# Four of eight convolution blocks per chunk: from the matrix engine to GpSimd, ScalarE and VectorE

## The chip, the core and the metric

The kernel runs on one core of a Trainium2 chip. A core has five engines, each with an instruction queue of its own that is worked off in order: TensorE (PE in the profile; its weight loads are the row PEld), VectorE (DVE), ScalarE (ACT), GpSimd (POOL) and SyncE (SP), which issues most of the transfers. The engines work on SBUF; TensorE writes its results to PSUM, which has eight banks of 512 fp32 values per partition. The metric is the device time of one execution in microseconds (us).

## The reference

Windowed attention for eight batches, eight heads, 576 positions, head width 64; behind it a feed-forward layer with a three-tap convolution along the sequence that gates the hidden units:

```
scores = (q @ k.T) / sqrt(64), masked to |i - j| <= 32
x = softmax(scores) @ v                      # (8, 576, 512) after the heads are put side by side
h = relu(x @ w_in)                           # (8, 576, 1024)
conv[s] = w0*h[s-1] + w1*h[s] + w2*h[s+1]    # per hidden unit, zeros outside
out = (h * sigmoid(conv)) @ w_out            # (8, 576, 512), fp32
```

## The kernel before, in words

The feed-forward part is cut into twelve chunks `c` of 384 positions; three chunks make two batches. A chunk has eight blocks `m` of 128 hidden units (partitions) by 384 positions. Each block goes through four steps: `ph` on TensorE (four matmuls with `w_in`, into a PSUM bank), `relu` on ScalarE (PSUM to the SBUF tile `hT`, with a factor 0.5), the convolution `pc` on TensorE (three matmuls whose weights are diagonal matrices `diag_w`, one for each tap, into another bank), then `tanh` on ScalarE in place in that bank and `gate` on VectorE (tanh plus one, times `hT`, into `gT`). Three groups `py` of eight matmuls then make the chunk's output, ScalarE copies each (`y`) and SyncE stores it. Chunks 0 and 1 are worked in halves of 192 positions.

Attention of batch `b` runs beside the chunks of the batches before it. GpSimd casts the loaded q, k and v to bf16 (`qb`, `kb`, `ve`), TensorE transposes q and k, ScalarE and VectorE copy these out (`qT`, `kT`), VectorE makes a shifted copy of v (`vo`, eight copies a batch), TensorE makes the scores, ScalarE the exponentials (`attn`), VectorE multiplies by the mask, TensorE multiplies with v, VectorE normalises (`rec`, `xn`), and for batches 2 to 7 a transposing DMA makes `xT`, the input of `ph`.

The order on every queue is fixed when the kernel is built. A `Planner` walks through all operations with costs given by hand and due times ("want"), takes on each engine the one that can start first and, among equals, the one due first, hands out the eight PSUM banks ("p"), and records the order. `shared` marks operations that it does not let run on DVE and POOL at once: all of POOL's, the mask multiplications and the `vo` copies. Chunk `c` is due at `S2 + (c - 2) * PC`; a batch is due `MO` or `ME` ahead of a chunk; `LD` spaces the loads. These times only sort the queues: on the chip every instruction starts when its own inputs and buffers are there. All calls go through a recording helper, so every instruction has line L209 in the profile (L212 in the changed file): operations are told apart by their tiles.

Of the kernel before, what the change touches and what calls it, by code (L numbers as in the profile page):

```python
# [10 lines left out]
FP32 = mybir.dt.float32  # L11
BF16 = mybir.dt.bfloat16
AF = mybir.ActivationFunctionType
ALU = mybir.AluOpType
# [12 lines left out]
class Planner:  # L27
# [110 lines left out]
def kernel(  # L138
# [21 lines left out]
    scale = 1.0 / float(D) ** 0.5  # L160
    CH = 2 * S // 3
    HW = CH // 2
    PAD = 32
    RP = S // 64
    NCH = 3 * B // 2
    ROWS = 2

    pp = ctx.enter_context(tc.tile_pool(name="pp", bufs=1))
    psum = ctx.enter_context(tc.tile_pool(name="psum", bufs=1, space=bass.MemoryType.PSUM))

# [14 lines left out]
    gT_pp = [pp.tile([128, MB, CH], BF16, name=f"gT{i}") for i in range(3)]  # L185
    rec_pp = [pp.tile([128, 8], FP32, name=f"rec{i}") for i in range(6)]
    y_pp = [pp.tile([128, d_model], FP32, name=f"y{i}") for i in range(6)]
    w_pp = [pp.tile([128, 1024], FP32, name=f"wst{i}") for i in range(4)]
    w_in_sb = pp.tile([128, KC, d_ff], BF16, name="w_in_sb")
    w_out_sb = pp.tile([128, MB, d_model], BF16, name="w_out_sb")  # L190
    conv_w_sb = pp.tile([128, 3, MB], FP32, name="conv_w_sb")
# [6 lines left out]
    pf = [psum.tile([128, 512], FP32, name=f"pf{i}") for i in range(8)]  # L198
# [46 lines left out]
    for t_ in ve_pp:  # L245
# [4 lines left out]
    vector.memset(hT_pp[1][:, :, HW + 1:HW + 3], 0.0)  # L250
    vector.memset(hT_pp[2][:, :, CH + 1], 0.0)

    plan = Planner({"p": range(8), "y": range(6),
                    "rec": range(6), "wst": range(4)})
# [238 lines left out]
    def taps(c, m, part, kk):  # L493
        kind = c % 3
        step = HW + (2 if kind == 1 else 0)
        base = hT_pp[kind][:, m, kk:kk + HW]
        return bass.AP(
            base.tensor, base.offset + step * (part or 0),
            [list(base.ap[0]), [step, 2 if part is None else 1], [1, HW]],
        )  # L500

    def pc_mm(c, m, part, ps):
        n = CH if part is None else HW
        for kk in range(3):
            tensor.matmul(
                pf[ps[0]][:, 0:n], diag_w[:, kk, m, :], taps(c, m, part, kk),
                start=(kk == 0), stop=(kk == 2),
            )

    def tanh(c, m, part, ps):  # L510
        n = CH if part is None else HW
        scalar.activation(pf[ps[0]][:, 0:n], pf[ps[0]][:, 0:n], AF.Tanh, bias=0.0, scale=1.0)

    def gate(c, m, part, ps):
        n = CH if part is None else HW
        o0 = HW * (part or 0)
        vector.scalar_tensor_tensor(
            out=gT_pp[c % 3][:, m, o0:o0 + n].rearrange("p (i x) -> p i x", x=HW),
            in0=pf[ps[0]][:, 0:n].rearrange("p (i x) -> p i x", x=HW), scalar=1.0,
            in1=taps(c, m, part, 1), op0=ALU.add, op1=ALU.mult,  # L520
        )
# [24 lines left out]

    PL = 0.25
    NSH = 8
    MO, ME = 5.0, 7.0
    NACT = 3  # L550
    LD = 1.7
    PC = 18.0
    S2 = 54.0

    def chunk_at(c):
# [2 lines left out]
    held = plan.held  # L558

    def ps_of(key):  # L560
        return held[key, "p"]
# [212 lines left out]
                    dma=0.75)  # L774


    def xt_need(c, part):
        x0, x1 = cols_of(c, part)
        b0 = c // 3 * 2
        need = []  # L780
        for b in range(2):
            lo, hi = max(x0, b * S) - b * S, min(x1, (b + 1) * S) - b * S
            if hi > lo:
                need += [("xt", b0 + b, x) for x in range(lo // 128, (hi - 1) // 128 + 1)]
        return need

    parts = {0: (0, 1), 1: (0, 1)}
    for c in range(NCH):
        ps_ = parts.get(c, (None,))
        for m in range(MB):  # L790
            for part in ps_:
                n = cols_of(c, part)[1] - cols_of(c, part)[0]
                w = CH if part is None else HW
                if c == 0:
                    t = 17.0 + 1.7 * m + 0.55 * part
                elif c == 1 and part == 0:
                    t = 18.1 + 1.7 * m
                elif c == 1:
                    t = 34.0 + 1.2 * m
                else:  # L800
                    t = chunk_at(c) + m * PC / (MB + 0.5)
                gap = (3.4 if c == NCH - 1 else 2.4) if part is None else 1.0
                hk, ck = ("ph", c, m, part), ("pc", c, m, part)
                add(hk, "PE", t, KC * (n / 2400.0 + 0.003),
                    lambda ps, c=c, m=m, part=part: ph_mm(c, m, part, ps),
                    xt_need(c, part) + [("w", 0, m // 2, h) for h in range(2)]
                    + [("gate", c - 3, m, p) for p in (None, 0, 1)],
                    lat=PL, takes=[("p", 1)])
                add(("relu", c, m, part), "ACT", t + 0.1, act(n),
                    lambda c=c, m=m, part=part: relu(c, m, part, ps_of(("ph", c, m, part))),  # L810
                    [hk] + [("gate", c - 3, m, p) for p in (None, 0, 1)]
                    + [("pc", c - 3, m, p) for p in (None, 0, 1)],
                    gives=[("p", hk, 0)])
                add(ck, "PE", t + gap, 3 * (w / 2400.0 + 0.003),
                    lambda ps, c=c, m=m, part=part: pc_mm(c, m, part, ps),
                    [("relu", c, m, part), *[("diag", m, kk) for kk in range(3)]]
                    + [("py", c - 3, i) for i in range(3)]
                    + ([("relu", c, m, 0)] if part == 1 and c % 3 == 0 else []),
                    lat=PL, takes=[("p", 1)])
                add(("tanh", c, m, part), "ACT", t + gap + 0.1, act(w),  # L820
                    lambda c=c, m=m, part=part: tanh(c, m, part, ps_of(("pc", c, m, part))),
                    [ck])
                add(("gate", c, m, part), "DVE", t + gap + 0.2, dve(w),
                    lambda c=c, m=m, part=part: gate(c, m, part, ps_of(("pc", c, m, part))),
                    [("tanh", c, m, part)] + [("py", c - 3, i) for i in range(3)],
                    gives=[("p", ck, 0)])
        for i in range(3):
            need = []
            for part in ps_:
                lo, hi = (0, CH) if part is None else (HW * part, HW * part + HW)  # L830
                if lo < 128 * i + 128 and hi > 128 * i:
                    need += [("gate", c, m, part) for m in range(MB)]
            last = c == NCH - 1 and i == 2
            nx = 2 if last else 1
            t = chunk_at(c + 1) + (2.7 + 2.6 * i) * PC / (MB + 0.5)
            yk = ("py", c, i)
            add(yk, "PE", t, MB * (d_model / 2400.0 + 0.003), lambda ps, c=c, i=i: py_mm(c, i, ps),
                need + [("w", 1, x, h) for x in range(4) for h in range(2)]
                + ([("issue", ("pc", c + 1, MB - 1, None))] if (c, i) == (NCH - 2, 2) else []),
                lat=PL, takes=[("p", nx)])  # L840
# [50 lines left out]
```

## Time and profile before

| what | value |
|---|---|
| time, median of 3 runs (lowest to highest) | 254.32 us (253.74 to 255.44) |
| the profiled execution: its time | 256.92 us |
| the profiled execution: its span, first to last instruction | 255.2 us |
| mean granted TensorE clock | 0.993 |
| last normalisation of batch 3, 5, 7 starts at | 97.4, 155.3, 211.2 us |

The span falls into three parts. Up to about 53 us the loads of the weights and of the first batches set the pace. From there to about 212 us attention of batches 2 to 7 runs beside chunks 1 to 9; three chunks and two batches take 58 and 56 us in the two full rounds (98 to 156 and 156 to 212 us). From 212 us on only the last chunks are left. PE's busy time is modelled: a matmul's recorded length contains the pipeline, so the pace of the matrix engine is read from start to start.

### The profile page before, as it was taken

The numbers are of one execution on the slowest core, as the hardware profiler recorded it, in microseconds if no ns is written. First come the engines' busy times: TensorE is split into PE (matmuls) and PEld (weight loads), VectorE is DVE, ScalarE is ACT, GpSimd is POOL, SyncE is SP. The second block draws the span as 40 slices with busy tenths as digits, with TensorE's granted clock in tenths as the row PEclk, the third lists the DMA queues.
The fourth block names the chain that finished last, engine by engine and source line by source line (L and its number), as shares of the span: only waits on it lengthen the run. The fifth ranks groups of instructions, "written<-read, shape, count | busy, mean of one in ns | idle before, by whom it ended". The sixth has DMA issues, their size and how long they took to land.

```text
span 255.2 us, 7176 instructions
## 1 busy us (share of the span) xinstructions
PE 240.9 (94%) x2782; PEld 154.2 (60%) x2782; DVE 179.6 (70%) x425; ACT 183.7 (72%) x429; POOL 76.4 (30%) x94
## 2 busy tenths in 40 slices
PE   7978998699999999999899999999999999999994
PEld 6976997586655555655555555656555555555542
DVE  4499789999997864649998958847798764233130
ACT  5789999387777776787568676776877775676651
POOL 5637676955300003055550065100560000000000
PEclk9999999799999999999999999999999999999999
DMA  6999999996614427899944699424995213321123
GB/s 240 273 267 388 237 318 405 215 352 176 158 42 59 119 59 222 163 308 313 315 121 63 179 347 214 111 83 137 367 181 84 94 45 65 109 85 41 41 83 127
DMA packets 69590, 45.96 MB, mean 180 GB/s; under 512 B 53532, under 2 KB 55860, under 8 KB 69556
## 3 DMA queue, kind: packets, MB, share of 16 engines
q1 hardware_dynamic: 69520, 45.49, 63.9%
q8 instruction: 22, 0.36, 0.6%
q14 instruction: 12, 0.10, 0.1%
q10 hardware_dynamic: 36, 0.01, 0.0%
HBM read 32.52 MB, written 9.44 MB: 164 GB/s over the span
## 4 chain that ended last, share of the span: by engine, by line
PE 60%; DVE 21%; DMA 8%; ACT 6%; issue 2%; POOL 1%; SPq 0%; DVEq 0%; POOLq 0%; ACTq 0%
PE pf L209 60%; DMA qst<-in_q_dram 6%; DVE kT L209 4%; DVE gT L209 4%; DVE xn L209 3%; DVE attn L209 3%; DVE vo L209 3%; ACT attn L209 3%; DVE qT L209 2%; DMA vst<-in_v_dram 2%; POOL qb L209 1%; DVE rec L209 1%; ACT diag_w L209 1%; ACT y L209 1%; ACT vo L209 1%
## 5 line engine op out<-in xcount | busy, mean ns | idle before, releaser
L209 DVE SCALAR_TENSOR_TENSOR gT<-pf,hT 128x384 bf16<-128x384 f32 (+1 forms) x112 | 57.0, 518 | 40.6 <-ACT pf L209 39.6
L209 PE MATMUL pf<-xT,w_in_sb 128*128 128x385 bf16 (+3 forms) x448 | 79.3, 305 | 0.5 <-ACT xT L209 0.4
L209 PE MATMUL pf<-w_out_sb,gT 128*128 128x512 bf16 (+1 forms) x296 | 67.6, 373 | 0.0
L209 PE MATMUL pf<-hT,diag_w 128*128 128x384 bf16 (+1 forms) x336 | 64.0, 303 | 1.4 <-DVE gT L209 1.2
L209 ACT ACTIVATE hT<-pf 128x385 bf16<-128x385 f32 (+3 forms) x112 | 50.7, 467 | 13.1 <-PE pf L209 11.1
L209 ACT ACTIVATE pf<-pf 128x384 f32<-128x384 f32 (+1 forms) x112 | 50.3, 457 | 5.1 <-PE pf L209 3.4
L209 PEld LDWEIGHTS <-w_in_sb 128*128 128x128 bf16 x448 | 39.4, 98 | 19.1 <-issue 0.5
L209 ACT COPY y<-pf 128x512 f32<-128x512 f32 (+1 forms) x36 | 20.9, 579 | 39.0 <-PE pf L209 39.0
L209 PEld LDWEIGHTS <-gT 128*128 128x128 bf16 x296 | 28.5, 98 | 29.3
L209 POOL TENSOR_SCALAR qb<-qst 128x1152 bf16<-128x1152 f32 x16 | 19.0, 1186 | 83.3 <-DMA qst<-in_q_dram 80.9
L209 ACT ACTIVATE attn<-pf 128x512 bf16<-128x512 f32 (+1 forms) x96 | 41.2, 506 | 1.2 <-PE pf L209 0.9
L209 PEld LDWEIGHTS <-diag_w 128*128 128x128 bf16 x336 | 30.6, 97 | 18.0 <-DVE gT L209 2.0
L209 DVE TENSOR_TENSOR attn<-attn,mask 128x1152 bf16<-128x1152 bf16 x32 | 27.4, 856 | 11.4 <-ACT attn L209 11.2
L209 POOL TENSOR_SCALAR ve<-vst 128x512 bf16<-128x512 f32 x40 | 26.1, 662 | 16.9 <-PE pf L209 6.1
L209 DVE TENSOR_TENSOR xn<-pf,rec 128x320 bf16<-128x320 f32 (+1 forms) x68 | 28.5, 461 | 0.1
L209 DVE COPY vo<-ve 64x520 bf16<-64x520 bf16 x60 | 24.7, 411 | 2.3 <-POOL ve L209 0.7
L209 DVE CAST qT<-pf 128x512 bf16<-128x512 f32 (+1 forms) x32 | 21.6, 717 | 5.2 <-PE pf L209 5.2
L209 DVE CAST kT<-pf 128x512 bf16<-128x512 f32 (+1 forms) x32 | 22.1, 725 | 2.2 <-PE pf L209 2.1
L209 POOL TENSOR_SCALAR kb<-kst 128x1152 bf16<-128x1152 f32 x16 | 19.1, 1192 | 9.9 <-DMA kst<-in_k_dram 9.6
L209 PEld LDWEIGHTS <-attn 128*64 128x64 bf16 x640 | 13.5, 115 | 12.1 <-issue 5.8
L209 PE MATMUL pf<-ve,attn 128*64 128x65 bf16 x384 | 17.0, 202 | 2.2 <-DVE attn L209 1.6
L209 PEld LDWEIGHTS <-kT 64*128 64x128 bf16 x576 | 10.5, 95 | 12.0 <-issue 6.7
(40 smaller groups left out, 173.0 us busy)
## 6 DMA issues: line engine op xcount, KB each, us to landing
qst<-in_q_dram SPq DMA_DIRECT2D x16, 576.0 KB, 6.6
kst<-in_k_dram SPq DMA_DIRECT2D x16, 576.0 KB, 7.9
out_dram<-y SPq DMA_DIRECT2D x35, 256.0 KB, 2.4
vst<-in_v_dram SPq DMA_DIRECT2D x24, 256.0 KB, 6.0
vst<-in_v_dram SPq DMA_DIRECT2D x16, 192.0 KB, 5.1
wst<-in_moe_w_in_dram SPq DMA_DIRECT2D x4, 512.0 KB, 6.3
wst<-in_moe_w_out_dram SPq DMA_DIRECT2D x4, 512.0 KB, 7.0
xT<-xn SPq DMA_TRANSPOSE x30, 2.5
```

Of the source, the lines that this page charges most:

```text
L209: return lambda *args, **kwargs: fixed(do(*args, **kwargs))
```

## The change

In chunks 2 to 10 the convolution of blocks 0, 1, 3 and 4 is no longer done by matmuls. Blocks 0 and 3 go to GpSimd: five instructions in SBUF, a multiplication into `ca` and two times a multiplication into `cb` and an addition to `ca`, in fp32; ScalarE's tanh then reads `ca` and writes a PSUM bank. Blocks 1 and 4 get a PSUM bank at once: ScalarE writes tap 0 times `hT` into it, VectorE adds taps 1 and 2 with two scalar_tensor_tensor instructions in place, tanh and gate follow as before. Blocks 2, 5, 6, 7 and the chunks 0, 1 and 11 stay with the matmuls. Four numbers of the planner change as well: PC, MO, ME and LD.

```diff
+    NCA = 3
+    ca_pp = [pp.tile([128, CH], FP32, name=f"ca{i}") for i in range(NCA)]
+    cb_pp = [pp.tile([128, CH], FP32, name=f"cb{i}") for i in range(2)]
...
+    def conv_pool(c, m, step, a, b):
+
+        a, b = halves(ca_pp[a]), halves(cb_pp[b])
+        if step in (0, 1, 3):
+            kk = (step + 1) // 2
+            pool.tensor_scalar(
+                out=b if step else a, in0=taps(c, m, None, kk), scalar1=conv_w_sb[:, kk, m:m + 1],
+                scalar2=None, op0=ALU.mult,
+            )
+        else:
+            pool.tensor_tensor(out=a, in0=a, in1=b, op=ALU.add)
+
+    def conv_acc(c, m, kk, ps):
+
+        to, w_ = halves(pf[ps[0]]), conv_w_sb[:, kk, m:m + 1]
+        if kk == 0:
+            scalar.activation(to, taps(c, m, None, kk), AF.Copy, bias=0.0, scale=w_)
+        else:
+            vector.scalar_tensor_tensor(
+                out=to, in0=taps(c, m, None, kk), scalar=w_, in1=to, op0=ALU.mult, op1=ALU.add
+            )
...
-    MO, ME = 5.0, 7.0
+    MO, ME = 6.0, 6.0
...
-    LD = 1.7
-    PC = 18.0
+    LD = 2.0
+    PC = 15.5
...
+    POOL_LAG = 6.0
+    BY_POOL, BY_DVE = (0, 3), (1, 4)
+
+    def conv_by(c, m):
+        if c < 2 or c == NCH - 1:
+            return "PE"
+        return "POOL" if m in BY_POOL else "DVE" if m in BY_DVE else "PE"
...
+                    add(tk, "ACT", t + POOL_LAG, act(w),
+                        lambda ps, c=c, m=m, qk=qk: tanh(c, m, None, ps, ca_pp[held[qk[0], "ca"][0]]),
+                        [ck], takes=[("p", 1)], gives=[("ca", qk[0], 0)])
```

What the planner makes of it, at three places. First GpSimd's queue at the casts of batch 5, which fall beside chunks 4 and 5 (`hT_89` is chunk 4's, `hT_90` chunk 5's). Before, the casts stand alone:

```order
L209 TENSOR_SCALAR ve_74<-vst 128x8x64 x5
L209 TENSOR_SCALAR qb_70<-qst_61 128x2x9x64
L209 TENSOR_SCALAR kb_72<-kst_63 128x2x9x64
L209 TENSOR_SCALAR qb_71<-qst_62 128x2x9x64
L209 TENSOR_SCALAR kb_73<-kst_64 128x2x9x64
L209 TENSOR_SCALAR ve_75<-vst 128x8x64 x5
```

The same casts in the changed kernel:

```order
L212 TENSOR_SCALAR ca_108<-hT_89,conv_w_sb 128x384
L212 TENSOR_SCALAR qb_70<-qst_61 128x2x9x64
L212 TENSOR_SCALAR cb_109<-hT_89,conv_w_sb 128x384
L212 TENSOR_TENSOR ca_108<-ca_108,cb_109 128x384
L212 TENSOR_SCALAR kb_72<-kst_63 128x2x9x64
L212 TENSOR_SCALAR cb_110<-hT_89,conv_w_sb 128x384
L212 TENSOR_SCALAR qb_71<-qst_62 128x2x9x64
L212 TENSOR_TENSOR ca_108<-ca_108,cb_110 128x384
L212 TENSOR_SCALAR ve_75<-vst 128x8x64 x2
L212 TENSOR_SCALAR ca_106<-hT_90,conv_w_sb 128x384
L212 TENSOR_SCALAR kb_73<-kst_64 128x2x9x64
```

A convolution that needs five instructions now has three casts between them, each of which waits for a load of its own.

Second VectorE's queue at the first mask multiplication of batch 4, beside the gates of chunk 4 (`gT_92`). Before:

```order
L209 TENSOR_TENSOR attn_82<-attn_82,mask 128x1152
L209 SCALAR_TENSOR_TENSOR gT_92<-pf_119,hT_89 128x384
L209 TENSOR_TENSOR attn_82<-attn_82,mask 128x1152
L209 COPY vo_76<-ve_74 64x520 x2
L209 SCALAR_TENSOR_TENSOR gT_92<-pf_120,hT_89 128x384
L209 COPY vo_76<-ve_74 64x520 x3
```

And in the changed kernel:

```order
L212 COPY vo_76<-ve_74 64x520 x2
L212 SCALAR_TENSOR_TENSOR pf_131<-hT_89,conv_w_sb,pf_131 128x384
L212 COPY vo_76<-ve_74 64x520
L212 SCALAR_TENSOR_TENSOR pf_131<-hT_89,conv_w_sb,pf_131 128x384
L212 COPY vo_76<-ve_74 64x520 x2
L212 TENSOR_TENSOR attn_82<-attn_82,mask 128x1152
L212 SCALAR_TENSOR_TENSOR gT_92<-pf_131,hT_89 128x384
```

The two additions of taps stand between the `vo` copies, and the mask now follows them.

Third ScalarE's queue in chunk 4, between exponentials of batch 4 (`attn`) and an output copy (`y_104`). Before:

```order
L209 ACTIVATE attn_82<-pf_126 128x512
L209 ACTIVATE hT_89<-pf_123 128x2x193
L209 ACTIVATE pf_120<-pf_120 128x384
L209 COPY y_104<-pf_124 128x512
L209 ACTIVATE hT_89<-pf_121 128x2x193
```

And in the changed kernel:

```order
L212 ACTIVATE attn_82<-pf_125 128x512
L212 ACTIVATE hT_89<-pf_129 128x2x193
L212 CAST qT_79<-pf_126 128x128x4
L212 ACTIVATE pf_125<-hT_89,conv_w_sb 128x384
L212 ACTIVATE pf_124<-ca_107 128x384
L212 ACTIVATE hT_89<-pf_127 128x2x193
L212 COPY y_104<-pf_131 128x512
```

`pf_125<-hT_89` is the new first tap, and `pf_124<-ca_107` is the tanh of a GpSimd block: the relu and the output copy behind it cannot start before GpSimd has finished that block.

More of the change, by code (lines that the diff above doesn't have):

```diff
@@ L251 @@
     vector.memset(hT_pp[2][:, :, CH + 1], 0.0)
-    plan = Planner({"p": range(8), "y": range(6),
+    plan = Planner({"p": range(8), "y": range(6), "ca": range(NCA), "cb": range(2),
                     "rec": range(6), "wst": range(4)})
@@ L508, in pc_mm, with halves, tanh @@
             )
-    def tanh(c, m, part, ps):
+    def halves(t_):
+        return t_[:, 0:CH].rearrange("p (i x) -> p i x", x=HW)
+    def conv_pool(c, m, step, a, b):
[16 more added lines that the diff above has]
+            )
+    def tanh(c, m, part, ps, from_=None):
         n = CH if part is None else HW
-        scalar.activation(pf[ps[0]][:, 0:n], pf[ps[0]][:, 0:n], AF.Tanh, bias=0.0, scale=1.0)
+        from_ = pf[ps[0]] if from_ is None else from_
+        scalar.activation(pf[ps[0]][:, 0:n], from_[:, 0:n], AF.Tanh, bias=0.0, scale=1.0)
     def gate(c, m, part, ps):
@@ L813 @@
                     gives=[("p", hk, 0)])
[L814 to L826, printed above, removed]
+                ready = ([("relu", c, m, part)] + [("py", c - 3, i) for i in range(3)]
+                         + ([("relu", c, m, 0)] if part == 1 and c % 3 == 0 else []))
+                how = conv_by(c, m)
@@ new lines @@
+                tk, gk = ("tanh", c, m, part), ("gate", c, m, part)
+                if how == "POOL":
+                    qk = [("pq", c, m, x) for x in range(4)] + [ck]
+                    for x in range(5):
+                        add(qk[x], "POOL", t + 0.5 + 0.01 * x, 0.95 if x in (2, 4) else 0.48,
+                            lambda *_, c=c, m=m, x=x, qk=qk: conv_pool(
+                                c, m, x, held[qk[0], "ca"][0],
+                                held[qk[1 if x < 3 else 3], "cb"][0] if x else 0),
+                            ready + qk[:x] + [("conv_w",)],
+                            takes=[("ca", 1)] if x == 0 else [("cb", 1)] if x in (1, 3) else [],
+                            gives=[("cb", qk[x - 1], 0)] if x in (2, 4) else [])
+                    add(tk, "ACT", t + POOL_LAG, act(w),
+                        lambda ps, c=c, m=m, qk=qk: tanh(c, m, None, ps, ca_pp[held[qk[0], "ca"][0]]),
+                        [ck], takes=[("p", 1)], gives=[("ca", qk[0], 0)])
+                    bk = tk
+                elif how == "DVE":
+                    bk = ("pq", c, m, 0)
+                    add(bk, "ACT", t + 0.4, act(w), lambda ps, c=c, m=m: conv_acc(c, m, 0, ps),
+                        ready + [("conv_w",)], takes=[("p", 1)])
+                    for kk in (1, 2):
+                        add(("pq", c, m, 1) if kk == 1 else ck, "DVE", t + 0.5 + 0.01 * kk, dve(w),
+                            lambda c=c, m=m, kk=kk, bk=bk: conv_acc(c, m, kk, ps_of(bk)),
+                            [("pq", c, m, kk - 1)])
+                    add(tk, "ACT", t + gap + 0.1, act(w),
+                        lambda c=c, m=m, bk=bk: tanh(c, m, None, ps_of(bk)), [ck])
+                else:
+                    bk = ck
+                    add(ck, "PE", t + gap, 3 * (w / 2400.0 + 0.003),
+                        lambda ps, c=c, m=m, part=part: pc_mm(c, m, part, ps),
+                        ready + [("diag", m, kk) for kk in range(3)], lat=PL, takes=[("p", 1)])
+                    add(tk, "ACT", t + gap + 0.1, act(w),
+                        lambda c=c, m=m, part=part: tanh(c, m, part, ps_of(("pc", c, m, part))), [ck])
@@ L827 @@
+                add(gk, "DVE", t + (POOL_LAG + 0.1 if how == "POOL" else gap + 0.2), dve(w),
+                    lambda c=c, m=m, part=part, bk=bk: gate(c, m, part, ps_of(bk)),
+                    [tk] + [("py", c - 3, i) for i in range(3)], gives=[("p", bk, 0)])
         for i in range(3):
```

## Prediction

> **What bounds the kernel now.** I read the head of the page first, then the chain of waits, then the busy time by stage, and last single stretches of the timeline. The head of the page, with its 40 slices (each digit is a busy share in tenths):
>
> ```profile
> span 255.2 us, 7176 instructions
> PE 240.9 (94%) x2782; PEld 154.2 (60%) x2782; DVE 179.6 (70%) x425; ACT 183.7 (72%) x429; POOL 76.4 (30%) x94
> PE   7978998699999999999899999999999999999994
> DVE  4499789999997864649998958847798764233130
> POOL 5637676955300003055550065100560000000000
> ```
>
> TensorE is full from slice 9 to the end. VectorE is also at nines in several slices (7 to 12, 19 to 21), and GpSimd works in bursts. The chain of waits, by engine, and three of its pieces:
>
> ```profile
> PE 60%; DVE 21%; DMA 8%; ACT 6%; issue 2%; POOL 1%; SPq 0%; DVEq 0%; POOLq 0%; ACTq 0%
> ...
> 117.15 5.90 DMA qst<-in_q_dram
> ...
> 175.10 4.71 DMA qst<-in_q_dram
> ...
> 181.06 5.15 DMA vst<-in_v_dram
> ```
>
> So PE is the bound, with VectorE as second. By stage (columns: stretch, length, then busy us and instructions of each engine):
>
> ```profile
> core 0: us, PE busy (x) PEld busy (x) DVE busy (x) ACT busy (x) POOL busy (x), PEclk, DMA share, GB/s
> 53.00:98.00 45.00, 44.17 (x571) 27.06 (x569) 38.48 (x91) 34.28 (x83) 7.75 (x9) 1.00 0.49 139
> 98.00:156.00 58.00, 56.05 (x618) 32.31 (x617) 43.89 (x96) 41.45 (x90) 21.87 (x23) 1.00 0.83 222
> 156.00:212.00 56.00, 55.61 (x619) 32.10 (x617) 43.39 (x97) 41.07 (x89) 10.80 (x14) 1.00 0.54 138
> 212.00:255.20 43.20, 39.62 (x222) 21.48 (x220) 11.45 (x21) 23.88 (x48) 0.00 (x0) 1.00 0.25 81
> ...
> 54.00:72.00 18.00, 17.61 (x235) 11.43 (x233) 17.20 (x40) 14.38 (x38) 7.75 (x9) 1.00 0.64 192
> 126.00:144.00 18.00, 18.00 (x235) 10.53 (x233) 16.84 (x43) 13.02 (x30) 4.26 (x6) 1.00 0.49 102
> ```
>
> In the attention stage, 53 to 212 us (159 us), PE is busy 44.17 + 56.05 + 55.61 = 155.8 us and DVE 38.48 + 43.89 + 43.39 = 125.8 us. In the last part DVE is nearly idle. Over 18 us DVE has reached 17.20 (95.6%) and 16.84 (93.6%).
>
> **What the change takes from TensorE.** The pace, from start to start:
>
> ```profile
> 134.84 0.83 PE L209 MATMUL pf<-xT,w_in_sb 128*128 128x385 bf16 x4
> 135.51 0.65 PE L209 MATMUL pf<-hT,diag_w 128*128 128x384 bf16 x3
> 136.00 0.38 PE L209 MATMUL pf<-w_out_sb,gT 128*128 128x512 bf16 x1
> ```
>
> Three convolution matmuls take 136.00 - 135.51 = 0.49 us, 0.163 each; four of `ph` take 0.67, 0.168 each. Nine chunks with four blocks of three matmuls: 108 go, 17.6 us. In PE's order 96 of them stood before the last attention matmul of batch 7; 12 stood after it, where 4 `ph` matmuls now come in addition. The attention stage loses 15.6 us of PE work and gives 0.7 to the end: 155.8 becomes 139.5. The end loses 2.0 and gains 0.7: -1.3. There PE has no rival (DVE 11.45 of 43.20 us), so I take -1.3 in full. Up to 53 us nothing of the change runs: 0, within 1 us either way for the new order of loads.
>
> **What it adds to VectorE.** Per block two scalar_tensor_tensor. Nearest row: the gate, the same operation on 384 elements with one operand in PSUM and one in SBUF.
>
> ```profile
> 133.83 0.56 DVE L209 SCALAR_TENSOR_TENSOR gT<-pf,hT 128x384 bf16<-128x384 f32 x1
> 134.30 0.18 DVE L209 RECIPROCAL rec<-pf 128x5 f32<-128x5 f32 x1
> ```
>
> It is 0.56 us long, but the next starts after 0.47. Most of the new ones have another instruction between them, so I take 0.47 (ends 0.47 and 0.56, which adds 2.7). In DVE's order 30 of the 36 stand before the last normalisation, and three gates fewer: 30 x 0.47 - 3 x 0.47 = +12.7 us.
>
> **What it adds to GpSimd, and what that does to VectorE.** The rows that bear on it (duration min/median/max in ns for the first two, then two groups of the stage 98 to 212 us, then two stretches of the timeline):
>
> ```profile
> L209 POOL TENSOR_SCALAR ve<-vst x40: 615/621/1215, 11.6 to 190.9; 128x512 bf16<-128x512 f32 x40
> L209 POOL TENSOR_SCALAR kb<-kst x16: 1151/1152/1753, 6.1 to 184.9; 128x1152 bf16<-128x1152 f32 x16
> ...
> L209 DVE TENSOR_TENSOR attn<-attn,mask 128x1152 bf16<-128x1152 bf16 x16 | 13.4, 839 | 7.0 <-ACT attn L209 6.9
> L209 DVE COPY vo<-ve 64x520 bf16<-64x520 bf16 x32 | 12.7, 398 | 1.5 <-POOL ve L209 0.7
> ...
> 114.28 2.35 POOL L209 TENSOR_SCALAR ve<-vst 128x512 bf16<-128x512 f32 x3
> 114.29 1.20 DVE L209 TENSOR_TENSOR attn<-attn,mask 128x1152 bf16<-128x1152 bf16 x1 [0.43 <-ACT attn L209]
> 115.52 1.25 DVE L209 COPY vo<-ve 64x520 bf16<-64x520 bf16 x2
> ...
> 136.53 0.29 DVE L209 COPY vo<-ve 64x520 bf16<-64x520 bf16 x1
> 136.85 0.76 DVE L209 TENSOR_TENSOR attn<-attn,mask 128x1152 bf16<-128x1152 bf16 x1
> ```
>
> GpSimd's rows give (1152 - 621) / 640 = 0.83 ns an element, so 0.515 us for a multiplication of 384. An addition with two inputs is not in the trace: 0.515 as lower end, one pass per input, 0.83, as upper; I take 0.83, since both inputs are fp32 tiles as wide as the casts' source. A block is 3 x 0.515 + 2 x 0.83 = 3.2 us; 15 of 18 fall in the stage: 48 us beside casts of 40.4, so 88 of 159 us, a share of 0.56 (before 0.25).
>
> At 114 us a mask multiplication beside GpSimd takes 1.20 instead of 0.76 us and a `vo` copy 0.62 instead of 0.29: +0.44 and +0.33, about 0.37 each, while GpSimd's casts are stretched from 0.62 to 0.78. Averaged over the stage the rows show +0.08 (839) and +0.11 (398), some 0.10. With GpSimd working 0.56 of the time I take 0.56 x 0.37 = 0.21; ends: 0, if its work falls into gaps as now, and 0.37. The stage has 71 such instructions: 71 x (0.21 - 0.10) = +7.8 us (0 to 19).
>
> The page "SBUF — State Buffer" of the Trainium skill (Who interferes with whom) has this as an exclusive lock: the later of the two waits until the earlier has ended, and a VectorE instruction with one SBUF input outside the two-port modes is not touched. By that rule the price is the rest of a whole GpSimd instruction, as taken; without it the stage's sum below would be 138.5 and PE would stay the bound. The stretch at 114 us agrees with the rule (1.20 against 0.76).
>
> **What it adds to ScalarE.** 15 first taps in the stage, and 15 tanh from SBUF. Nearest rows:
>
> ```profile
> L209 ACT ACTIVATE pf<-pf 128x384 f32<-128x384 f32 x80 | 39.4, 493 | 4.5 <-PE pf L209 2.8
> ...
> L209 ACT ACTIVATE diag_w<-ident,conv_w_sb 128x128 bf16<-128x128 bf16 x24 | 8.1, 396 | 1.5 <-DVE conv_w_sb L209 1.5
> ```
>
> The first tap lies between 0.40 (the scaled copy from SBUF at 128 elements) and 0.62; at 0.6 and 0.1 more per tanh, ScalarE has 116.8 + 10.5 = 127 of 159 us. It is not the bound, but its queue can be held up (below).
>
> **The sum.** VectorE in the stage: 125.8 + 12.7 + 7.8 = 146.3 us, against PE's 139.5. VectorE becomes the bound. Two things cost nothing in this sum. A GpSimd block lies 6 us of due time ahead of its tanh and is covered by the other blocks' matmuls; if that cover is gone, rival three gives the price. A VectorE block holds its PSUM bank from the first tap to the gate, two VectorE instructions longer (about 1 us); seven other banks cover that, and without them `ph` would wait that 1 us once a block, up to 15 us in all. It can't be full: I take the lower of the two shares it has shown, 93.6%, because it must hold for 150 us and not 18. 146.3 / 0.936 = 156.3, that is -2.7 on 159 us; the end gives -1.3; together -4.0. The loads move one or two stores earlier in SP's queue, with the transposes of their batch: 0, since the two loads on the chain keep their distance. The profiled execution took 256.92 us (span 255.2 and 1.7 around it), 1% over the median of the runs; the same difference taken from the median: 254.3 - 4.0 = 250.3 us. Ends: no contention at 95.6% is 138.5 / 0.956 = 144.9, -15.4 in all, 238.9; contention of 0.37 everywhere at 93.6% is 157.7 / 0.936 = 168.5, +8.2, 262.5.
>
> **Rivals.** One: PE stays the bound, because GpSimd's work falls into gaps; all 17.6 us come off, 236.7 us. For it: PE's row of nines, DVE's 24% of idle time. Against: 146.3 against 139.5. Two: the gain of the stage is eaten, because VectorE never gets over 92%; 146.3 / 0.92 = 159.0, only the end remains, 253. For it: in 53 to 98 us it had 85.5%. Three, slower: GpSimd's queue becomes a chain. Casts wait for loads there:
>
> ```profile
> POOL qb L209 <- DMA qst<-in_q_dram: 80.9, 11, 29.0
> qst<-in_q_dram SPq DMA_DIRECT2D x16, 576.0 KB, 6.6
> ```
>
> Until now this wait held nothing but casts. Now convolution instructions stand behind it, ScalarE's tanh waits for them, and relu, exponentials and output copies stand behind that tanh. The planner leaves 6 us between a block's `ph` and its tanh, of which 3.2 are the block itself: it decides as soon as a load is more than 2.8 us late at its cast. The chain spends 5.90, 4.71 and 5.15 us on loads, 5.3 on average. If each of batches 3 to 7 loses 5.3 - 2.8 = 2.5 us on that path, 250.3 + 12.5 = 263; two of five give 255. I put it at 259. Against it: the planner orders the casts by the same times as before.
>
> **How the numbers follow.** VectorE as bound with a small gain (244 to 254, most likely 250.3): 0.45. Everything gained (about 237): 0.12. Gain eaten (252 to 257): 0.18. Slower by GpSimd's queue (255 and more): 0.25. One per cent, 2.5 us, is about what a measurement of this kernel can tell from no change; the limits are 251.8 and 256.9. Faster: 0.12 + 0.39 = 0.51. Same: 0.06 + 0.15 = 0.21. Slower: 0.25 + 0.03 = 0.28. The range leaves out most of rival one and the tail of rival three: 241 to 260.
>
> **What would show it.** DVE over 92% busy from 53 us to the last normalisation and PE's row broken by eights and sevens; `vo` copies near 0.50 us and masks near 0.97 on average; GpSimd's addition near 0.83 us; on the chain less PE and more DVE. Wrong would be: DVE still waiting for ACT most of all, with ACT waiting for POOL's `ca` (rival three), or PE at nines throughout (rival one). An addition of over 1.5 us, or a first tap that holds ScalarE for over 0.7 us, would break the sum upwards.

## The result, and the profile after

| | before | after |
|---|---|---|
| median of 4 runs (lowest to highest) | 254.66 us (253.74 to 255.44) | 263.37 us (261.49 to 264.99) |
| ratio after to before, 95% interval | | 1.034 (1.025 to 1.043) |
| the profiled execution: time, span | 256.92, 255.2 us | 261.49, 259.8 us |

The kernel became slower by 3.4%. The forecast was 250.3 us with a range of 241 to 260, so the time lies outside it, on the side of rival three. The profiled execution of the changed kernel is the fastest of its four, and that of before lies above all four of its runs, so the two traces, both at a mean granted TensorE clock of 0.993, show 4.6 us of the 8.7 us between the medians. The other three runs of the changed kernel, 262.4, 264.3 and 265.0 us, had a lower clock (0.98, 0.967 and 0.96). Ratios and their intervals, here and below, leave out executions that ran over 1.5% longer than the fastest of the same kernel; medians keep them.

From the page of the changed kernel: the head, the three rows of slices, the chain by engine, and six groups (busy us, mean ns of one, idle time before them with what ended it).

```profile
span 259.8 us, 7053 instructions
PE 227.6 (88%) x2674; PEld 143.8 (55%) x2674; DVE 202.3 (78%) x461; ACT 188.7 (73%) x447; POOL 181.1 (70%) x184
...
PE   7888997899898799879997899599978998978994
...
DVE  4687899999989977699997997979889975544230
...
POOL 5638756956497199999999699949997098691000
...
DVE 31%; POOL 26%; PE 25%; issue 6%; ACT 6%; DMA 4%; POOLq 0%; SPq 0%; DVEq 0%; ACTq 0%
...
L212 POOL TENSOR_SCALAR cb<-hT,conv_w_sb 128x384 f32<-128x384 bf16 x36 | 47.2, 1313 | 0.0
L212 POOL TENSOR_SCALAR ca<-hT,conv_w_sb 128x384 f32<-128x384 bf16 x18 | 23.5, 1305 | 28.5 <-ACT hT L212 24.0
L212 POOL TENSOR_TENSOR ca<-ca,cb 128x384 f32<-128x384 f32 x36 | 37.4, 1039 | 1.7
...
L212 DVE COPY vo<-ve 64x520 bf16<-64x520 bf16 x60 | 29.3, 489 | 2.0 <-POOL ve L212 0.3
...
L212 DVE TENSOR_TENSOR attn<-attn,mask 128x1152 bf16<-128x1152 bf16 x32 | 29.2, 920 | 1.3 <-ACT attn L212 1.2
...
L212 ACT ACTIVATE pf<-ca 128x384 f32<-128x384 f32 x18 | 8.9, 494 | 21.0 <-POOL ca L212 19.1
```

TensorE's row of nines is broken, as forecast, but the engine that has most nines now is GpSimd (from slice 15 on), and it holds 26% of the chain, where it had 1%. The groups say why: one multiplication takes 1.31 us on average where the forecast had 0.515, one addition 1.04 where it had 0.83. The 90 convolution instructions take 47.2 + 23.5 + 37.4 = 108.1 us, 6.0 us a block instead of 3.2. The last group shows who waits: ScalarE stood idle for 19.1 us in front of tanh instructions whose `ca` was not ready. The busy time by stage, in the stretches of the prediction (the third a microsecond longer, up to the last normalisation):

```profile
core 0: us, PE busy (x) PEld busy (x) DVE busy (x) ACT busy (x) POOL busy (x), PEclk, DMA share, GB/s
53.00:98.00 45.00, 40.96 (x524) 24.25 (x523) 40.33 (x93) 31.91 (x75) 29.57 (x27) 1.00 0.59 166
98.00:156.00 58.00, 51.30 (x584) 29.17 (x582) 51.38 (x108) 43.40 (x96) 54.61 (x53) 1.00 0.82 211
156.00:213.00 57.00, 50.14 (x566) 28.37 (x565) 50.81 (x107) 41.68 (x91) 44.90 (x43) 0.97 0.48 126
213.00:259.80 46.80, 39.70 (x216) 20.84 (x214) 16.79 (x31) 26.18 (x56) 17.87 (x16) 1.00 0.23 75
```

From 98 to 156 us GpSimd is busy 54.61 of 58 us (94%), more than any other engine. VectorE has 40.33 + 51.38 + 50.81 = 142.5 of 160 us in the attention stage (89%) and TensorE 142.4: VectorE has less work than forecast (146.3), TensorE 2.9 us more (139.5), and neither fills its time. Who waits for whom, the waits of the changed kernel show (us in total, times, longest):

```profile
DVE gT L212 <- ACT pf L212: 32.7, 32, 2.4
POOL ca L212 <- ACT hT L212: 24.0, 6, 7.7
ACT pf L212 <- POOL ca L212: 19.1, 14, 2.4
...
POOL qb L212 <- DMA qst<-in_q_dram: 6.1, 6, 1.7
```

VectorE waits most of all for ScalarE's tanh, as it did before (39.6 us), and ScalarE waits for GpSimd fourteen times. GpSimd hardly waits for the loads of q any more: 6.1 us in six pieces of at most 1.7, where it was 80.9 us in eleven (the loads of k and v together: 11.7 us, before 14.7). What a cast of q waits for now is mostly what stands ahead of it in its own queue. A stretch of GpSimd's timeline (start, us, instruction) has no gap:

```profile
98.63 1.25 POOL L212 TENSOR_SCALAR cb<-hT,conv_w_sb 128x384 f32<-128x384 bf16 x1
99.85 1.15 POOL L212 TENSOR_SCALAR kb<-kst 128x1152 bf16<-128x1152 f32 x1
100.97 1.00 POOL L212 TENSOR_TENSOR ca<-ca,cb 128x384 f32<-128x384 f32 x1
101.94 1.15 POOL L212 TENSOR_SCALAR qb<-qst 128x1152 bf16<-128x1152 f32 x1
103.07 1.25 POOL L212 TENSOR_SCALAR cb<-hT,conv_w_sb 128x384 f32<-128x384 bf16 x1
104.28 1.15 POOL L212 TENSOR_SCALAR kb<-kst 128x1152 bf16<-128x1152 f32 x1
105.40 1.00 POOL L212 TENSOR_TENSOR ca<-ca,cb 128x384 f32<-128x384 f32 x1
```

A multiplication of 384 elements takes longer here than a cast of 1152, both under the name TENSOR_SCALAR. At the other end of this stretch, ScalarE's timeline (the wait in brackets):

```profile
103.54 0.48 ACT L212 ACTIVATE pf<-pf 128x384 f32<-128x384 f32 x1
106.43 0.49 ACT L212 ACTIVATE pf<-ca 128x384 f32<-128x384 f32 x1 [2.41 <-POOL ca L212]
```

The addition that ends at 106.40 releases the tanh at 106.43; a copy of `kT` and two `hT` stood behind it. The last place is the end. In the chain of the changed kernel, in order of time:

```profile
206.66 0.52 ACT hT L212
207.27 1.60 POOL ca L212
...
218.70 1.01 POOL ca L212
220.16 0.45 ACT pf L212
```

Two blocks follow each other on GpSimd for 12.4 us with nothing else in the chain, and the next two do the same from 223.0 to 234.7 us. The start of the last normalisation, read from the row of `rec` (start of the first and of the last), was 210.7 us before and 212.1 after:

```profile
L209 DVE RECIPROCAL rec<-pf x68: 145/173/196, 21.2 to 210.7; 128x5 f32<-128x5 f32 x48, 128x4 f32<-128x4 f32 x20
```

```profile
L212 DVE RECIPROCAL rec<-pf x68: 144/177/386, 19.6 to 212.1; 128x5 f32<-128x5 f32 x48, 128x4 f32<-128x4 f32 x20
```

So up to there the change costs 1.4 us, and behind it 259.8 - 212.1 = 47.7 against 255.2 - 210.7 = 44.5 us, 3.2 more: together the 4.6 us between the two traces.

### The profile page after: what moved, and what is told of

Read it like the earlier page. It is cut to its first block, busy times and chain, and to the rows that moved or that the text cites. A ratio compares the mean times of both kernels' runs of the same rounds, so it can differ in the third digit from the quotient of the medians.

```text
span 259.8 us, 7053 instructions
## 1 busy us (share of the span) xinstructions
PE 227.6 (88%) x2674; PEld 143.8 (55%) x2674; DVE 202.3 (78%) x461; ACT 188.7 (73%) x447; POOL 181.1 (70%) x184
## 4 chain that ended last, share of the span: by engine, by line
DVE 31%; POOL 26%; PE 25%; issue 6%; ACT 6%; DMA 4%; POOLq 0%; SPq 0%; DVEq 0%; ACTq 0%
PE pf L212 25%; POOL ca L212 11%; POOL cb L212 10%; DVE gT L212 6%; DVE vo L212 6%; DVE kT L212 5%; DVE xn L212 4%; DVE attn L212 4%; DVE qT L212 4%; POOL ve L212 3%; DMA qst<-in_q_dram 3%; DVE pf L212 2%; ACT pf L212 2%; POOL qb L212 1%; ACT attn L212 1%
## 5 line engine op out<-in xcount | busy, mean ns | idle before, releaser
L212 DVE SCALAR_TENSOR_TENSOR gT<-pf,hT 128x384 bf16<-128x384 f32 (+1 forms) x112 | 56.3, 519 | 33.7 <-ACT pf L212 32.7
L212 PE MATMUL pf<-w_out_sb,gT 128*128 128x512 bf16 (+1 forms) x296 | 69.5, 380 | 3.7 <-DVE gT L212 2.1
L212 ACT ACTIVATE pf<-pf 128x384 f32<-128x384 f32 (+1 forms) x94 | 40.7, 442 | 10.7 <-DVE pf L212 5.9
L212 PE MATMUL pf<-hT,diag_w 128*128 128x384 bf16 (+1 forms) x228 | 40.9, 292 | 7.6 <-ACT hT L212 5.0
L212 POOL TENSOR_SCALAR cb<-hT,conv_w_sb 128x384 f32<-128x384 bf16 x36 | 47.2, 1313 | 0.0
L212 POOL TENSOR_SCALAR ca<-hT,conv_w_sb 128x384 f32<-128x384 bf16 x18 | 23.5, 1305 | 28.5 <-ACT hT L212 24.0
L212 POOL TENSOR_TENSOR ca<-ca,cb 128x384 f32<-128x384 f32 x36 | 37.4, 1039 | 1.7
L212 DVE COPY vo<-ve 64x520 bf16<-64x520 bf16 x60 | 29.3, 489 | 2.0 <-POOL ve L212 0.3
L212 PEld LDWEIGHTS <-diag_w 128*128 128x128 bf16 x228 | 20.0, 97 | 18.7 <-issue 9.9
L212 DVE SCALAR_TENSOR_TENSOR pf<-hT,conv_w_sb,pf 128x384 f32<-128x384 bf16 x36 | 22.4, 621 | 2.5 <-ACT pf L212 2.2
L212 ACT ACTIVATE pf<-ca 128x384 f32<-128x384 f32 x18 | 8.9, 494 | 21.0 <-POOL ca L212 19.1
```

Source lines behind the costliest of these rows:

```text
L212: return lambda *args, **kwargs: fixed(do(*args, **kwargs))
```

## The experiments

The theory from this profile: GpSimd's instructions are dear, and its queue became the chain. What had to be told apart: the dear part of the change from the harmless ones, the reason why the multiplication is dear, and whether GpSimd costs by its results being late, by VectorE's stretched instructions, or by late casts. Unless another length is named, a difference is one of ratios to the kernel before, taken in the same session; a point is 1% of that kernel, about 2.55 us.

| label | what it is | median us | ratio to before (95%) |
|---|---|---|---|
| e4_plan_only | planner's new numbers alone | 256.9 | 1.001 (0.997 to 1.005) |
| e2_dve_only | ACT/DVE blocks alone | 250.5 | 0.975 (0.965 to 0.985) |
| e3_pool_only | GpSimd blocks alone | 275.2 | 1.069 (1.059 to 1.079) |
| e1_imm | changed, multiplication by a constant in place of the tap weights, second operation | 243.5 | 0.948 (0.941 to 0.954) |
| e8_two_ops | changed, tap weight kept, second operation | 244.5 | 0.958 (0.952 to 0.964) |
| e6_pool_one | changed, one GpSimd block a chunk | 254.3 | 0.993 (0.989 to 0.998) |
| e10_one_two_ops | the same with second operation | 248.5 | 0.975 (0.969 to 0.982) |
| e7_plan_true | changed, planner given the measured prices | 268.0 | 1.045 (1.033 to 1.056) |
| e9_unused | GpSimd's work done, but read by nobody | 258.3 | 1.012 (1.004 to 1.019) |
| e14_unused_two_ops | the same with second operation | 252.4 | 0.989 (0.982 to 0.996) |
| e11_three | e8 without one ACT/DVE block | 251.7 | 0.987 (0.980 to 0.994) |

### The parts alone: e4, e2, e3

One line decides which block goes where; everything else of the change stays.

```diff
-    BY_POOL, BY_DVE = (0, 3), (1, 4)
+    BY_POOL, BY_DVE = (), ()          # e4
+    BY_POOL, BY_DVE = (), (1, 4)      # e2
+    BY_POOL, BY_DVE = (0, 3), ()      # e3
```

> No block is moved; only the planner's numbers PC, MO, ME, LD are those of the changed kernel. Theory that the new due times are the loss: 258 us or more. Both other theories: 252 to 257 us, no change that can be measured.

> Only blocks 1 and 4 are moved (ScalarE and VectorE); blocks 0 and 3 go back to the matmuls; the planner's numbers are those of the changed kernel. Theory GpSimd: 54 matmuls less and no new queue, so faster than before: 246 to 252 us. Theory VectorE: 12.7 us more on VectorE bring no gain or a loss: 254 to 260 us.

> Only blocks 0 and 3 are moved (GpSimd); blocks 1 and 4 go back to the matmuls. Theory GpSimd: slower than before, 257 to 264 us, with ScalarE waiting for ca and GpSimd's row at nines. Theory VectorE: VectorE has 12.7 us less to do than in the changed kernel, so 248 to 254 us.

The planner's numbers do nothing (1.001). ScalarE's and VectorE's blocks alone gain 2.5 points (1.5 to 3.5), so all of the loss comes with GpSimd's blocks. These alone cost 6.9 points, more than was expected. The changed kernel, which has the ACT/DVE blocks in addition, loses 3.5 points less, where these blocks by themselves gain 2.5. Part of that may be another thing: all four runs had a mean granted clock of 0.951 to 0.975, and its trace has slices in which the clock falls (tenths of full speed):

```profile
PEclk9999997799999999599999997999999997986999
```

What share of the 6.9 points goes with the clock was not separated; e3 is taken for its sign alone.

### Is the multiplication's price the cause: e1

```diff
-                out=b if step else a, in0=taps(c, m, None, kk), scalar1=conv_w_sb[:, kk, m:m + 1],
-                scalar2=None, op0=ALU.mult,
+                out=b if step else a, in0=taps(c, m, None, kk), scalar1=0.5,
+                scalar2=0.0, op0=ALU.mult, op1=ALU.add,
```

> GpSimd's multiplications of the convolution take a constant (times 0.5 plus 0.0, the operation of the casts) instead of a weight per partition; the tap weights of blocks 0 and 3 are left out. Theory GpSimd (its multiplication takes 1.24 us where 0.515 was reckoned, so its queue became the bound): if the weight per partition is what makes it dear, the multiplication falls to about 0.5 us, a block from 5.7 to 3.6 us, and the time falls by 8 us or more, to 248 to 255 us. If the types (bf16 in, fp32 out) make it dear, it stays at 1.24 and the time at 261 to 265. Theory VectorE (VectorE with its additions and the shared port is the bound, whatever one GpSimd instruction takes): the time stays above 258 even if the multiplication gets cheap.

The multiplications fell to 0.57 to 0.59 us and the time to 243.5 us, 0.948 of before: under all that was expected, and past the 250.3 us of the forecast. So the price of the multiplication alone turns a loss of 3.4 points into a gain of 5.2. But the edit changed two things at once: a constant in place of the weight of each partition, and a second operation. Which of the two makes it cheap, it can't say.

### Which form is dear: e5

Behind the last convolution 48 instructions on scratch tiles were added, four of each form, so that the price of a form stands alone (the time of this kernel, 301.0 us in its one run, means nothing).

```diff
+    def probe(to, src, n, by, two, src1=None):
+        for _ in range(4):
...
+                pool.tensor_scalar(
+                    out=to[:, 0:n], in0=src[:, 0:n], scalar1=by, scalar2=0.0 if two else None, op0=ALU.mult,
+                    **({"op1": ALU.add} if two else {}),
+                )
...
+    probe(ca_pp[0], bsrc, 384, wt, False)
+    probe(cb_pp[0], bsrc, 384, 0.5, False)
+    probe(w_pp[1], bsrc, 384, 0.5, True)
...
+    probe(y_pp[0], bsrc, 384, wt, True)
```

> The changed kernel with 48 GpSimd instructions on scratch tiles behind its last convolution, four of each form, where VectorE has little left to do. Its time says nothing (it is longer by the added instructions); the lengths of the forms are wanted. If the weight per partition is dear by the element: 1.24 us with it whatever the types and whether it has one or two operations, about 0.5 without, 0.65 at 192 elements and 3.2 at 1024. If it is dear by the instruction: about 0.9 at 192 and 1.8 at 1024. If the single operation (no second one) is dear: the constant with one operation is also 1.24, and the weight with two is near 0.55. If the types are: bf16 in and out, or fp32 in and out, differ from bf16 in and fp32 out. The addition of two fp32 inputs: 1.0 at 384, 0.55 at 192.

GpSimd's timeline (start, us for four). TENSOR_SCALAR rows with `conv_w_sb` multiply by the weight of each partition, the others by a constant; the TENSOR_TENSOR row adds two fp32 inputs; the rows of 246.23 and 295.79 have the second operation.

```profile
236.10 5.26 POOL L212 TENSOR_SCALAR ca<-mask,conv_w_sb 128x384 f32<-128x384 bf16 x4
241.34 4.93 POOL L212 TENSOR_SCALAR cb<-mask 128x384 f32<-128x384 bf16 x4
246.23 2.30 POOL L212 TENSOR_SCALAR wst<-mask 128x384 f32<-128x384 bf16 x4
248.51 5.26 POOL L212 TENSOR_SCALAR ca<-wst,conv_w_sb 128x384 f32<-128x384 f32 x4
253.75 5.26 POOL L212 TENSOR_SCALAR xn<-mask,conv_w_sb 128x384 bf16<-128x384 bf16 x4
258.99 3.34 POOL L212 TENSOR_SCALAR cb<-mask,conv_w_sb 128x192 f32<-128x192 bf16 x4
...
273.94 11.33 POOL L212 TENSOR_SCALAR wst<-wst 128x1024 f32<-128x1024 f32 x4
...
287.78 4.20 POOL L212 TENSOR_TENSOR ca<-wst 128x384 f32<-128x384 f32 x4
...
295.79 2.64 POOL L212 TENSOR_SCALAR y<-mask,conv_w_sb 128x384 f32<-128x384 bf16 x4
```

Four rows of the same size and types make a table of two by two, as steps from start to start: with one operation 5.26 / 4 = 1.31 us (weight) and 1.23 (constant), with two operations 0.66 (weight) and 0.57 (constant). A step holds a short gap; the instructions themselves are 1.245, 1.170, 0.588 and 0.513 us long (mean of four each), and the last is the 0.515 us that the forecast read off the casts. The weight costs 0.08 to 0.09 us; the second operation takes away 0.65. Of the types tried none matters: 1.31 with fp32 in, and with bf16 out. From 192 to 384 elements the single form grows from 0.83 to 1.31 us, 2.5 ns an element, three times the 0.83 ns that the prediction read off the casts; at 1024 elements it takes 2.83 with a constant. The instruction that does less arithmetic is the slower one; why that is, no run here shows. The casts of this kernel, from which the forecast took its price, have two operations.

The Trainium skill's page "GPSIMD Engine Reference" (Engine selection) puts GpSimd at about half VectorE's pace for operations with two inputs and roughly at line rate for one input. The order of the rows is the other way for the single form: a step of 1.23 to 1.31 us with one input against 4.20 / 4 = 1.05 for the addition with two. The measurement decides.

### The second operation in place: e8

```diff
-                scalar2=None, op0=ALU.mult,
+                scalar2=0.0, op0=ALU.mult, op1=ALU.add,
```

> The changed kernel with one difference: GpSimd's multiplication keeps its weight per partition and gets a second operation, plus 0.0. Theory of the single operation (it is the missing second operation that costs 1.24 us, not the weight): the multiplication falls to 0.57 to 0.66 us and the time to that of the run with constants, 241 to 246 us. Theory of the weight: the multiplication stays above 1.1 us and the time at 260 us or more.

The arithmetic is the changed kernel's, weights and all, and the planner's input is the same, so the order of every queue is too. 244.5 us, 0.958 of before, and the best version that computes the reference; against the changed kernel it is 7.6 points, some 19 us. The clock is not the reason: at 0.993 and 0.98 the changed kernel took 261.5 and 262.4 us, at 0.998 and 0.979 this one took 243.2 and 244.6. From its page, then by stage:

```profile
PE   7797999499989989999998899989999899999994
...
PE 42%; DVE 38%; ACT 10%; DMA 4%; issue 3%; SPq 1%; POOL 0%; DVEq 0%; ACTq 0%
...
L212 DVE TENSOR_TENSOR attn<-attn,mask 128x1152 bf16<-128x1152 bf16 x32 | 30.7, 968 | 1.5 <-ACT attn L212 1.4
...
L212 DVE COPY vo<-ve 64x520 bf16<-64x520 bf16 x60 | 25.3, 422 | 2.1 <-POOL ve L212 0.5
...
L212 POOL TENSOR_SCALAR cb<-hT,conv_w_sb 128x384 f32<-128x384 bf16 x36 | 22.7, 631 | 0.0
```

```profile
53.00:95.00 42.00, 39.98 (x545) 25.36 (x548) 39.34 (x95) 33.90 (x82) 22.47 (x27) 1.00 0.55 158
95.00:149.00 54.00, 51.18 (x588) 29.76 (x593) 50.50 (x109) 44.81 (x99) 44.12 (x55) 1.00 0.91 240
149.00:201.00 52.00, 48.56 (x563) 28.16 (x569) 49.76 (x108) 41.12 (x92) 34.06 (x44) 1.00 0.50 138
```

GpSimd has left the chain (26% to 0%), and ScalarE's tanh no longer waits for `ca`. In the stage VectorE has 39.34 + 50.50 + 49.76 = 139.6 of 148 us, 94.3%: about the share of 93.6% that the prediction took, with less work than its 146.3. But TensorE is as full, 139.7 us or 94.4%; its row is at nines almost throughout, which the prediction had named as the sign of rival one, and its share of the chain is 42% against 38%. Which of the two bounds this kernel was not settled; in e1 TensorE has 28% of the chain and VectorE 50%.

### Fewer GpSimd blocks, and the planner: e6, e10, e7

e6 and e10 keep one GpSimd block a chunk, `BY_POOL = (0,)`, e6 with the dear form (one operation), e10 with the cheap one (e8's edit). e7 is the changed kernel with prices told to the planner as measured:

```diff
-    POOL_LAG = 6.0
+    POOL_LAG = 9.0
...
-                        add(qk[x], "POOL", t + 0.5 + 0.01 * x, 0.95 if x in (2, 4) else 0.48,
+                        add(qk[x], "POOL", t + 0.5 + 0.01 * x, 1.05 if x in (2, 4) else 1.3,
```

> Block 0 alone goes to GpSimd, blocks 1 and 4 to ScalarE and VectorE, block 3 back to the matmuls. Theory GpSimd (its queue bounds): its work falls from 105 to 52 us, well under the other queues; VectorE bounds as in the kernel with constants: 244 to 249 us. Theory that any GpSimd block on ScalarE's queue is the loss: half of the loss stays, 254 us or more.

> Block 0 alone on GpSimd, with the second operation; otherwise as the run with one block, which took 254.3 us. Theory that the price of the multiplication is the loss: 246 to 249 us, between the kernel without a GpSimd block (250.5) and the one with two cheap blocks (243.5). Theory that any GpSimd block on ScalarE's queue costs: 253 us or more.

> The changed kernel, but the planner reckons 1.3 us for GpSimd's multiplication and 1.05 for its addition, and has the tanh due 9 us after the block's first matmul instead of 6; the order of the queues changes, the work does not. Theory GpSimd's sum of work is the loss: within 3 us of the changed kernel, 259 to 266 us. Theory that the loss is the order made with wrong prices (ScalarE held up by late blocks): 254 us or less.

e6 was expected at 244 to 249 by the sum of GpSimd's work, and missed: 254.3. That would fit the theory that any GpSimd block costs, but e10, at 248.5, does not. GpSimd was busy for only 87.2 of the 152 us of its stage (57%), and yet the dear form costs 0.993 - 0.975 = 1.8 points, 4.6 us, against e10. In e6 ScalarE waits for `ca`, 8.0 us in all, and in e10 not at all. So GpSimd need not be full to be dear. That the delay of five instructions in a row, with casts in between, reaches ScalarE is a part of it; how large a part, these two runs can't say, since the dear form also costs where nobody reads it (next section). And one cheap GpSimd block (e10, 0.975) gains nothing over none (e2, 0.975); only two do.

e7 does not repair the change (1.045 against 1.034, with intervals that overlap), and its 268.0 us lie above both expectations: a later tanh and true prices don't win the loss back. Its trace shows more. The chain by engine:

```profile
PE 39%; DVE 33%; DMA 9%; ACT 6%; POOL 5%; SPq 4%; issue 3%; POOLq 0%; DVEq 0%; ACTq 0%
```

GpSimd's share of the chain falls from 26% to 5%, and in front of the 18 tanh of its blocks ScalarE waits 0.0 us instead of 19.1. Yet the last normalisation starts at 221.8 us, 9.7 later than in the changed kernel, while the end is 43.4 us against 47.7. So the wait on ScalarE is one form that the delay takes: when the planner makes room for it, the time is lost elsewhere. Where is open; the profiled run's clock was also lower (0.966 against 0.993).

### Work that nobody reads: e9, e14

GpSimd does the five instructions of blocks 0 and 3 into scratch, and matmuls make the convolution of these blocks as in e2. e14 is the same with e8's edit.

```diff
+                    how = "PE"
...
-                elif how == "DVE":
+                if how == "DVE":
```

> GpSimd does all its work of the changed kernel, with the dear multiplication, into ca and cb, but nobody reads it: blocks 0 and 3 are convolved by matmuls as before, blocks 1 and 4 by ScalarE and VectorE. Beside it stands the kernel without GpSimd's work at 250.5 us. If the loss is that ScalarE waits for ca (and all behind it in its queue), the time is within 3 us of that: 248 to 254 us. If the loss is that GpSimd delays VectorE at the shared port and its own casts, it is 258 us or more. In between, both have a part, in the ratio of the distances.

> GpSimd's work is done with the second operation and nobody reads it; blocks 0 and 3 are convolved by matmuls. Beside it stand the kernel without GpSimd's work at 250.5 us and the one with the dear, unused work at 258.3. If it is the length of GpSimd's instructions that delays the casts and VectorE, 250 to 253 us. If any work at all on GpSimd does it, 255 us or more.

The head and the `vo` copies of e9, then of e14:

```profile
PE 232.6 (91%) x2703; PEld 150.0 (59%) x2728; DVE 202.0 (79%) x461; ACT 189.7 (74%) x447; POOL 181.9 (71%) x184
...
L212 DVE COPY vo<-ve 64x520 bf16<-64x520 bf16 x60 | 29.7, 495 | 5.9 <-POOL ve L212 4.4
```

```profile
PE 231.7 (92%) x2728; PEld 148.6 (59%) x2728; DVE 201.7 (80%) x461; ACT 189.5 (75%) x447; POOL 147.3 (59%) x184
...
L212 DVE COPY vo<-ve 64x520 bf16<-64x520 bf16 x60 | 26.0, 433 | 2.0 <-POOL ve L212 0.4
```

e9's 258.3 us lie at the edge of the second expectation, GpSimd's disturbance of others, and e14's 252.4 us in the first. Against e2, work that nobody reads costs 3.7 points in the dear form, so GpSimd disturbs others by more than its late results; in the cheap form it is 1.4, with intervals that just overlap. VectorE's busy time is 194.8 us in e2, 201.7 in e14 and 202.0 in e9: it is stretched by about 7 us, by as much in the cheap form as in the dear one. The 2.2 points between e14 and e9 are therefore not more stretching, and not the clock, which was 0.98 to 0.993 in both. What the rows show there is waiting: the `vo` copies wait 4.4 us for the casts `ve` in e9 and 0.4 in e14. That these late casts are all of the 2.2 points was not shown.

### One ACT/DVE block less: e11

```diff
-    BY_POOL, BY_DVE = (0, 3), (1, 4)
+    BY_POOL, BY_DVE = (0, 3), (1,)    # with e8's edit
```

> Blocks 0 and 3 on GpSimd with the second operation, block 1 on ScalarE and VectorE, block 4 back to the matmuls. If VectorE is the bound of the kernel with two cheap blocks (95% busy there), a block less on it gains up to 4 us: 240 to 243 us. If TensorE is as near, the 27 matmuls that come back cost 4.4 us: 245 to 248 us.

With block 4 back on TensorE 251.7 us came out, slower than either expectation and 2.9 points slower than e8. VectorE has 194.4 us of work instead of 199.2, TensorE 227.2 instead of 223.0, so neither sum explains it; the `vo` copies went up to 0.51 us from 0.42, which may come from another order of casts and copies. The cause is open.

## Why the prediction was wrong

The step that failed is the price of a GpSimd block, "A block is 3 x 0.515 + 2 x 0.83 = 3.2 us". The multiplication was read off casts, which are the same operation in name but have two arithmetic operations where the new one has one: it takes 1.31 us on average in the changed kernel and 1.24 at least, and alone, in e5, it is 1.245 us long, so contention is not the reason. With additions of 1.04 a block is 6.0 us. The multiplication had no range at all. The addition had the bounds 0.515 and 0.83, both taken from the casts, and came out above them. Putting in the second operation, and nothing else, moves the time from 1.034 to 0.958 of before (e8). That the price is the cause is shown; by which way it reaches the end of the kernel is shown in part (below).

The other steps:

- **The cover of a GpSimd block.** "6 us of due time ahead of its tanh", minus 3.2, left 2.8 us. With 6.0 nothing is left, and casts stand in between. ScalarE then waits 19.1 us. The sum had this at nothing.
- **Rival three** had the right chain (GpSimd's queue, then ScalarE's tanh, then everything behind it) and the wrong cause. It wanted late loads at the casts; these waits shrank from 80.9 to 6.1 us. Its 259 us was a price of late loads and is no estimate of what happened. The sign that the prediction gave for it, DVE waiting for ACT most of all (32.7 us) and ACT for `ca` (19.1 us), did appear, but it can't tell late loads from dear instructions.
- **How the loss divides.** Between e8 and the changed kernel lie 7.6 points. With the results unread the same difference of form costs 2.2 (e14 to e9). So about 5.4 points come only when someone reads `ca`. This takes the two effects as additive, which was not tested. In the changed kernel they show as ScalarE's waits and as a longer end; but e7, without these waits and with a shorter end, is no faster, so they are not two costs that could be taken away one by one.
- **TensorE loses 17.6 us and is no longer the bound**: right for the changed kernel, with 108 matmuls fewer, 142.4 us in the stage against 139.5 forecast, and 25% of the chain instead of 60%.
- **VectorE as the next bound at 93.6%**: the share comes out once the multiplication is cheap (e8: 94.3%; e1: 140.38 of the 147 us from 53 to 200, 95.5%); in the changed kernel it was at 89%, waiting. That VectorE is then the bound is not shown: in e8 TensorE is as full, and taking a block off VectorE (e11) made the kernel slower. For rival one the prediction put DVE's idle time at 24%; in the stage from 53 to 212 us it was 33.2 of 159 us, 21%.
- **VectorE's added work.** 142.5 us in the changed kernel, 139.6 in e8, against 146.3. The contention term of +7.8 was for a GpSimd share of 0.56. In the stage of e8, at a share of 0.68, masks went from 819 to 974 ns (24) and `vo` from 403 to 406 (48), 3.9 us; in the changed kernel, at 0.81, 903 and 527 give 7.7 us, which meets the forecast by luck. The additions of taps had a pace of 0.53 us (from 135.28 to 135.81, for one), not 0.47, which goes the other way; what else made the sum too high was not found.
- **The end, -1.3 us**: +3.2 in the changed kernel, where GpSimd's blocks of chunks 9 and 10 stand in the chain. In e8 it was 242.9 - 199.7 = 43.2 against 44.5, -1.3 as forecast.
- **ScalarE's first tap**, 0.6: measured 0.598. The tanh from SBUF takes 0.494, like that from PSUM (0.493), so the 0.1 added for it was not there.
- **Planner's numbers at nothing**: right (e4, 1.001).

The signs named at the end watched the addition ("over 1.5 us would break the sum"); it came out at 1.04, and the instruction that broke the sum was the one for which the trace seemed to have a row.

## What to carry to other kernels

A price may be taken from a row only if the whole form is the same, and the number of arithmetic operations in the instruction belongs to the form; where a new instruction will run dozens of times, a few scratch copies of it at the end of the kernel give its price before anything is built on it. Work moved to a slow engine is judged by the delay of its chain in that engine's queue as well as by its sum: at 57% busy (e6) GpSimd's dear form still cost 1.8 points, and an order that hides the delay from one engine (e7) need not save any time. And an experiment that changes two things at once (e1) shows that a remedy exists, not which of the two it is.

## What the runs showed of the hardware that was not expected

- On GpSimd a tensor_scalar of 384 elements takes 1.23 to 1.31 us from start to start with one operation and 0.57 to 0.66 with two (e5); the types tried made no difference and the weight of each partition costs under 0.1 us.
- GpSimd work that nobody reads still costs a kernel bound by VectorE and TensorE: 1.4 points with 73 us of it in the changed kernel's places (e14, intervals that just overlap), 3.7 with 109 us (e9).
- The time of the changed kernel goes with the granted clock from run to run (261.5 us at 0.993, 265.0 at 0.96), and the two slowest kernels of the table had a low clock in every run (e3: 0.951 to 0.975, e7: 0.947 to 0.966). Whether waiting lowers the clock was not tried.
